# Attention in 64x64 blocks, local scores shelved by four transfers, and new orders: a four-layer attention kernel on one core

## The chip, the core and the metric

The kernel runs on one core of a Trainium2 chip. A core has five engines that work side by side, each through its own list of instructions in order: PE (matrix products, with PEld for the loading of weights), DVE and ACT (elementwise work and reductions), POOL (slower elementwise work) and SP, which does nothing here but issue DMA transfers. Data lie in DRAM, in an on-chip memory of 128 partitions (SBUF), and in eight banks that PE writes and DVE and ACT read (PSUM). The metric is the device time of one execution in microseconds (us), the median of several runs; less is better.

## What is computed

Four residual layers follow each other on one sequence of 2048 positions and 512 channels, in 32 heads of 16 channels: A, B, A, B. Layer A is local: each query sees 8 keys, at its own position and at every second position before it. Layer B is a causal window of 256 keys.

```python
    def _A_ref(x, wqkv, wo):
        B, S, D = x.shape
        H = 32; Dh = D // H
        W, dil = 8, 2
...
        off = jnp.arange(W) * dil
        idx = pos[:, None] - off[None, :]
        mask = idx >= 0
...
        logits = jnp.einsum("bhsd,bhswd->bhsw", q, kg) * scale
        logits = jnp.where(mask[None, None, :, :], logits, -1e9)
        attn = _softmax(logits, axis=-1)
        o = jnp.einsum("bhsw,bhswd->bhsd", attn, vg)
        return (lambda x, *d: x.transpose(*d))(o, 0, 2, 1, 3).reshape(B, S, D) @ wo

    def _B_ref(x, wqkv, wo):
        B, S, D = x.shape
        H = 32; Dh = D // H; W = 256
...
        scores = jnp.einsum("bhqd,bhkd->bhqk", q, k) * (Dh ** -0.5)
        idx = jnp.arange(S)
        mask = (idx[:, None] - idx[None, :] >= 0) & (idx[:, None] - idx[None, :] < W)
        scores = jnp.where(mask[None, None], scores, -1e9)
        p = _softmax(scores, axis=-1)
        o = jnp.einsum("bhqk,bhkd->bhqd", p, v)
        return (lambda x, *d: x.transpose(*d))(o, 0, 2, 1, 3).reshape(B, S, D) @ wo

    x = A_x
    x = x + _A_ref(_layernorm(x, axis=-1), A_wqkv, A_wo)
    x = x + _B_ref(_layernorm(x, axis=-1), B_wqkv, B_wo)
    x = x + _A_ref(_layernorm(x, axis=-1), A_wqkv, A_wo)
    x = x + _B_ref(_layernorm(x, axis=-1), B_wqkv, B_wo)
    return x
```

## The kernel before

The sequence is cut into 8 chunks of 256 positions. A pass takes a layer A and the layer B behind it through the chunks, so there are 16 periods, each with one chunk of A (`layer_a`) and one of B (`layer_b`); in time, A of the next chunk runs beside B of the last.

**Order.** The code doesn't run in the order in which it is written. Every step is added to a plan as a task with an engine, a price in us, the values that it reads and writes, and buffers with a count. A table `ORDER` has a place for every task, in its engine's list; a negative place moves the task to its other engine (`alt`, DVE instead of POOL for instance). `Plan.order()` replays these lists against the prices, and the instructions are recorded in the order that it gives. On the chip each engine takes its list strictly in order, SP too: a transfer that waits for data holds up all transfers behind it.

**Layer A, the way of the local scores.** PE computes for 32 queries at a time the scores against a window of 39 keys (L1153, the X tasks), for two halves t of the chunk. ACT copies them to a buffer `s` (L1161, two copies a half; the pool `psc` has two such buffers). `shelve` writes them to DRAM as `sd` (L1169), and `band` reads back only the 8 keys of each query (L1173, `l`), by a pitch that slides along the window. DVE takes the maximum (L1192), ACT the exponential, and the weights go out to DRAM (`ptd`, L1237) and come back spread (`pt`, L1243). PE mixes the values with them (L1260). In SP's list the read back stands behind its shelving and waits for its landing.

**Layer B.** Queries and keys of four 16-channel parts are stacked in tiles `stk`. For each quarter j of the heads there is first a pass for the row maxima: 8 units, each a score unit of 128 queries by 384 keys for two heads (L1354, L1357), a DVE step that folds the last 128 columns onto the first 128 through a triangular mask (`pick`, L1375), and a reduction over 256 columns (L1371). The maxima go through DRAM into `stk`, and the same products are made anew, transposed, with the maximum subtracted (L1447, L1449). For a group of four heads (`hh`, eight groups a chunk) and for each of the two key chunks b there are two score units, two exponentials of 128x768 on ACT (L1453) into a buffer `p` (pool `pp6`, three buffers), one POOL instruction that zeroes what lies outside the band (L1462), and eight products with the values (L1479) into one PSUM bank `acc`, which two groups share and ACT then copies out (L1515). In the first chunk of a layer there are no keys before it and half of this falls away. A key block is 128 keys against 256 queries, or 128 against 128, in which two corners of 64x64 are empty.

The lines of the shelving and of the read back; `sd.t` has 4 rows of 32 queries, `S_.t` 128 partitions of 39 x 32 numbers (`WIN` is 39, `H` 32):

```python
            def shelve(S_=S_, sd=sd):
                nc.sync.dma_start(sd.t[:, 0 : 32 * WIN * H].rearrange("g (q x) -> g q x", q=32), S_.t.rearrange("p k s -> p (k s)"))
...
            plan.add("SP", 0.4, shelve, r=vS, w=[vsd], size=650)
            plan.add("SP", 0.4, band, r=[vsd], w=[vL[t]], size=160)
```

## Time and profile before

| what | value |
|---|---|
| median of 3 runs | 1647.87 us (1644.64 to 1656.72) |
| the profiled execution, its time | 1659.09 us |
| its span, first to last instruction | 1657.3 us |
| mean granted clock of PE | 0.909 |
| PE's idle time by the span less its busy time | 271.4 us |

The profile is one execution. A row of a group says how long its instructions kept the engine busy, how long one took on average, and how long the engine stood idle just before them and for whom. The chain is the work that ended last, followed back from the end. A window's row has the busy time of each engine in a stretch, then the granted clock of PE (1.00 is full speed), the busy share of the 16 DMA engines and GB/s. PE in 40 slices of the span, its clock and the DMA share, in tenths:

```profile
PE   8779779699697978979698797978969799696987
...
PEclk9789999799798998989888898989979899797999
DMA  9665353444535446353354634545353564524341
```

The dips of PE come back once in two or three slices, that is once in a period of some 100 us.

### The profile page before, as it was taken

The page shows a single profiled execution, that of the slowest core. Times are in us where ns is not written, and L with a number is a line of the kernel's source. Part 1 is how long each engine was busy: PE and PEld are TensorE (multiplying, and loading weights), DVE is VectorE, ACT ScalarE, POOL GpSimd, SP SyncE. Part 2 cuts the span into 40 slices and gives each one's busy share as a digit, 9 for nine tenths or more (in the row PEclk, how much of TensorE's full clock was granted, in tenths as well). Part 3 has the DMA queues.
Part 4 walks back from the last instruction along what each step waited for, and adds up shares of the span by engine and source line. Part 5 has one row for each costly group of instructions (what it writes and reads, how often), then busy time and mean ns, then how long its engine had stood idle before and what let it go on. Part 6 is the DMA issues. An engine that isn't in the chain of part 4 may idle for free.

```text
span 1657.3 us, 49223 instructions
## 1 busy us (share of the span) xinstructions
PE 1385.9 (84%) x20958; PEld 840.1 (51%) x20958; DVE 856.1 (52%) x1768; ACT 879.8 (53%) x1343; POOL 408.6 (25%) x478
## 2 busy tenths in 40 slices
PE   8779779699697978979698797978969799696987
PEld 7555546356373554636355363644637356363533
DVE  7445464463645626365462526537453463545664
ACT  6533547366364654637465272755636465364554
POOL 4330113132031322213121031313222131121333
PEclk9789999799798998989888898989979899797999
DMA  9665353444535446353354634545353564524341
GB/s 267 166 138 144 103 120 90 126 119 127 130 105 122 114 132 116 117 147 108 91 118 125 136 103 139 119 129 124 109 111 96 142 131 121 135 80 124 81 118 54
DMA packets 181397, 202.09 MB, mean 122 GB/s; under 512 B 90269, under 2 KB 120733, under 8 KB 181177
## 3 DMA queue, kind: packets, MB, share of 16 engines
q1 hardware_dynamic: 180920, 198.68, 46.4%
q8 instruction: 164, 2.69, 0.7%
q14 instruction: 57, 0.46, 0.1%
q10 hardware_dynamic: 256, 0.26, 0.1%
HBM read 101.97 MB, written 79.36 MB: 109 GB/s over the span
## 4 chain that ended last, share of the span: by engine, by line
PE 49%; DMA 28%; DVE 6%; issue 5%; SPq 5%; ACT 5%; POOL 1%; ACTq 0%; POOLq 0%; DVEq 0%
DMA sd<-s 11%; PE banks L1007 7%; PE banks L1479 6%; PE banks L1008 6%; PE banks L1009 6%; PE banks L1029 4%; PE banks L1027 4%; DMA pt<-ptd 3%; PE banks L1030 3%; PE banks L1447 3%; PE banks L1153 2%; ACT p L1453 2%; PE banks L1354 2%; PE banks L1260 2%; DMA stk<-re 2%
## 5 line engine op out<-in xcount | busy, mean ns | idle before, releaser
L1453 ACT ACTIVATE p<-banks,sclB 128x768 f32<-128x768 f32 x480 | 415.8, 902 | 203.1 <-PE banks L1449 185.9
L1462 POOL TENSOR_SCALAR_AFFINE_SELECT p<-p 128x1024 f32<-128x1024 f32 x240 | 261.3, 1097 | 873.8 <-ACT p L1453 843.2
L1375 DVE COPY_PREDICATED banks<-maskt,banks 128x256 f32<-128x256 int16 x448 | 185.4, 425 | 238.1 <-PE banks L1357 208.0
L1371 DVE TENSOR_REDUCE m<-banks 128x2 f32<-128x512 f32 x448 | 302.7, 689 | 9.6
L1479 PE MATMUL banks<-p,v 128*32 128x256 f32 (+1 forms) x3840 | 206.5, 351 | 32.8 <-POOL p L1462 15.6
L1354 PE MATMUL banks<-stk,stk 48*128 48x128 f16 (+1 forms) x896 | 118.9, 261 | 85.2 <-DMA stk<-re 32.8
L1447 PE MATMUL banks<-stk,stk 64*128 64x256 f16 x960 | 132.4, 284 | 51.4 <-DVE m L1371 33.7
L1479 PEld LDWEIGHTS banks<-p,v 128*32 128x32 f32 x3840 | 113.4, 115 | 118.2 <-issue 55.6
L1357 PE MATMUL banks<-stk,stk 48*128 48x256 f16 (+1 forms) x1024 | 131.5, 258 | 14.1 <-DMA stk<-re 5.9
L1354 PEld LDWEIGHTS <-stk 48*128 48x128 f16 x896 | 51.7, 96 | 179.2 <-issue 120.7
L1447 PEld LDWEIGHTS <-stk 64*128 64x128 f16 x960 | 55.6, 95 | 126.2 <-issue 92.0
L1291 DVE SCALAR_TENSOR_TENSOR el<-banks,eh 128x512 f16<-128x512 f32 x64 | 43.1, 689 | 126.5 <-ACT eh L1288 88.4
L1449 PE MATMUL banks<-stk,stk 64*128 64x128 f16 x960 | 107.2, 222 | 0.0
L1192 DVE TENSOR_REDUCE mx<-l 128x64 f32<-128x512 f32 x32 | 32.9, 1027 | 137.5 <-DMA l<-sd 99.1
L1260 PE MATMUL banks<-pt,vs 39*32 39x64 f32 x4096 | 62.9, 251 | 39.2 <-DMA pt<-ptd 19.5
L1161 ACT COPY s<-banks 128x624 f32<-128x624 f32 x64 | 74.7, 1260 | 38.6 <-PE banks L1153 38.6
L1260 PEld LDWEIGHTS banks<-pt,vs 39*32 39x32 f32 x4096 | 52.6, 114 | 50.1 <-issue 28.6
L1008 PE MATMUL banks<-xl,wA1h 128*128 128x256 f16 x256 | 70.8, 277 | 1.0 <-issue 1.0
L1007 PE MATMUL banks<-xh,wA1h 128*128 128x256 f16 x256 | 70.9, 277 | 0.4 <-DMA xh<-ht 0.4
L1007 PE MATMUL banks<-xh,wA0h 128*128 128x256 f16 x256 | 71.2, 278 | 0.1
L1007 PE MATMUL banks<-xh,wB0h 128*128 128x256 f16 x256 | 71.2, 278 | 0.0
L1008 PE MATMUL banks<-xl,wA0h 128*128 128x256 f16 x256 | 71.0, 277 | 0.0
(202 smaller groups left out, 2851.3 us busy)
## 6 DMA issues: line engine op xcount, KB each, us to landing
stk<-re SPq DMA_DIRECT2D x256, 96.0 KB
sd<-s SPq DMA_DIRECT2D x32, 624.0 KB
pt<-ptd SPq DMA_DIRECT2D x64, 312.0 KB
re<-eh SPq DMA_DIRECT2D x128, 128.0 KB
vs<-vd SPq DMA_DIRECT2D x64, 156.0 KB
vd<-ve SPq DMA_DIRECT2D x32, 256.0 KB
xm<-y SPq DMA_DIRECT2D x32, 256.0 KB
re<-el SPq DMA_DIRECT2D x64, 128.0 KB
```

Source lines behind the costliest of these rows:

```text
L1007: nc.tensor.matmul(ps[mp].t[:, i], wh, xh, start=k == 0, stop=False)
L1008: nc.tensor.matmul(ps[mp].t[:, i], wh, xl, start=False, stop=False)
L1260: nc.tensor.matmul(acc.t[32 * r : 32 * r + 32, bb].rearrange("p (a x q u) -> p a x q u", a=2, q=16, u=2)[:, :, 2 * m + b2], vs.t[k, b2, 32 ...
L1354: nc.tensor.matmul(ps.t[:, par, 0 : (2 - qb) * P], lhs, stk[hf, bef][r, col, qb * P :], start=True, stop=True)
L1357: nc.tensor.matmul(ps.t[:, par, (2 - qb) * P : 3 * P], lhs, stk[hf, now][r, col, : (1 + qb) * P], start=True, stop=True)
L1371: nc.vector.tensor_reduce(out=m.t[:, :, u, qb], in_=ps.t[:, :, 0 : 2 * P], op=ALU.max, axis=AX.X)
L1375: nc.vector.copy_predicated(t[:, :, 0:P], maskt[:, 0:P].bitcast(I16).unsqueeze(1).broadcast_to([P, 2, P]), t[:, :, 2 * P : 3 * P])
L1447: nc.tensor.matmul(o[:, two], k[:, jf * P : (jf + 1) * P], q, start=True, stop=True)
L1449: nc.tensor.matmul(o[:, one_], k[:, jo * P : (jo + 1) * P], q[:, qo * P : (qo + 1) * P], start=True, stop=True)
L1453: nc.scalar.activation(pt.t[:, :, 2 * i : 2 * i + 2].rearrange("p s m q -> p m s q"), ps.t[:, :, : 3 * P].rearrange("p m (s q) -> p m s q" ...
L1462: nc.gpsimd.affine_select(out=v, in_=v, pattern=[[0, 8], [-1 if b == 0 else 1, P]], compare_op=ALU.is_gt if b == 0 else ALU.is_ge, fill=0. ...
L1479: nc.tensor.matmul(o, v[:, jj, 17 * h : 17 * h + 32], rhs, start=z == 0 and (b == 0 or first), stop=z == 1 and b == 1, tile_position=(0, 3 ...
```

## The change

Three things change together.

1. `shelve` issues four transfers, one for each 32 partitions, instead of one. The pool `psc` goes from two buffers to one.
2. In chunks after the first, layer B works in blocks of 64 keys by 64 queries and leaves out those outside the band. A row-max unit runs over 320 columns for each 64 queries instead of 384 (`halves`), and the fold over 64 columns instead of 128. A group's scores come as two wide units of 448 columns and one thin unit, each PE instruction over a quarter of the array (64 rows by 64 columns); the exponentials become two of 128x896 and one of 128x768. The masks become two for a group, each either four POOL selects of 64x256 or one DVE copy. The values are 16 wide and 16 thin products on half the rows, into two banks, so that the two halves have to be added: one ACT copy and one DVE addition a group, instead of one ACT copy for two groups.
3. The table `ORDER` is another one throughout, and some prices of the plan are others: the shelving's, and that of the gather `get` (L1243), whose size goes from 1015 to 1350.

```diff
 ORDER = {
-    "S": [15, 11, 0, 1, 3, 2, 33, 16],
-    "pA": [2, -1, 3, -2, 2, 22, 4, 30, 8, 10, 11, 9, 10, 5, 8, 4, -4, 7, 31, 9, 39, 12, 32, -14, 16, 11, 15, 6, 13, 9,
...
+    "S": [16, 13, 12, 0, 11, 7, 6, 35, 19],
...
-    for name, bufs in (("px", 4), ("pqm", 1), ("pk", 1), ("psc", 2), ("pl", 1), ("ppt", 1), ("pvs", 1), ("pve", 1), ("po4", 1), ("pos", 2), ("pxn", 2),
-                       ("pxt", 2), ("pp6", 3), ("pqk", 2), ("poh", 2), ("ps1", 1), ("psm", 2)):
+    for name, bufs in (("px", 4), ("pqm", 1), ("pk", 1), ("psc", 1), ("pl", 1), ("ppt", 1), ("pvs", 1), ("pve", 1), ("po4", 1), ("pos", 2), ("pxn", 2),
+                       ("pxt", 2), ("pp6", 2), ("pp7", 2), ("pqk", 2), ("poh", 2), ("ps1", 1), ("psm", 2)):
...
             def shelve(S_=S_, sd=sd):
-                nc.sync.dma_start(sd.t[:, 0 : 32 * WIN * H].rearrange("g (q x) -> g q x", q=32), S_.t.rearrange("p k s -> p (k s)"))
+                for g in range(4):
+                    nc.sync.dma_start(sd.t[g, 0 : 32 * WIN * H].rearrange("(q x) -> q x", q=32), S_.t[32 * g : 32 * g + 32].rearrange("p k s -> p (k s)"))
...
-            plan.add("SP", 0.4, shelve, r=vS, w=[vsd], size=650)
+            plan.add("SP", 1.9, shelve, r=vS, w=[vsd], size=450)
...
+                    def halves(u=u, qb=qb, ps=ps, hf=hf, hp=hp):
+                        col = 4 * hp + u
+                        for part in range(2):
+                            for h in range(2):
+                                for par in range(2):
+                                    r = slice(64 * par, 64 * par + 48)
+                                    n = C - qb * P - 64 * h
+                                    lhs = stk[hf, 0][r, col, qb * P + 64 * h : qb * P + 64 * h + 64]
+                                    o = ps.t[64 * h : 64 * h + 64, par, 0:320]
+                                    o, k = (o[:, 0:n], stk[hf, bef][r, col, C - n :]) if part == 0 else (o[:, n:], stk[hf, now][r, col, : 320 - n])
+                                    nc.tensor.matmul(o, lhs, k, start=True, stop=True, tile_position=(64 * par, 64 * h))
...
                     def pick(ps=ps):
                         t = ps.t
-                        nc.vector.copy_predicated(t[:, :, 0:P], maskt[:, 0:P].bitcast(I16).unsqueeze(1).broadcast_to([P, 2, P]),
-                                                  t[:, :, 2 * P : 3 * P])
+                        nc.vector.copy_predicated(t[:, :, 0:64], trm[:, 0].bitcast(I16).unsqueeze(1).broadcast_to([P, 2, 64]), t[:, :, C : C + 64])
...
+                def score(ps, at, i, pieces, hh=hh, hf=hf):
+                    col = 2 * (hh % 4) + i
+                    for n in range(2):
+                        for h in range(2):
+                            for par in range(2):
+                                r = slice(64 * par, 64 * par + 64)
+                                kt, k0, q0, q1, x0 = pieces[h][n]
+                                nc.tensor.matmul(ps.t[64 * h : 64 * h + 64, par, at + x0 : at + x0 + q1 - q0], stk[hf, kt][r, col, k0 : k0 + 64],
+                                                 stk[hf, 0][r, col, q0:q1], start=True, stop=True, tile_position=(64 * par, 64 * h))
+
+                wide_ = (((now, 0, 0, 256, 0), (bef, 128, 0, 192, 256)), ((bef, 192, 0, 256, 192), (now, 64, 64, 256, 0)))
+                thin_ = (((now, 128, 128, 256, 0), (bef, 0, 0, 64, 128)), ((bef, 64, 0, 128, 64), (now, 192, 192, 256, 0)))
...
+                def mask(E, x, n):
+                    if E is nc.vector:
+                        v = x.t[:, :, 0:64]
+                        p, m, z = (list(y) for y in v.ap)
+                        v = bass.AP(tensor=v.tensor, offset=v.offset, ap=[p, m, [n - 64, 2], z])
+                        E.copy_predicated(v, trm[:, 1:3].bitcast(I16).unsqueeze(1).broadcast_to([P, 4, 2, 64]),
+                                          nul.unsqueeze(1).unsqueeze(1).broadcast_to([P, 4, 2, 64]))
+                        return
+                    for h in range(2):
+                        r = slice(64 * h, 64 * h + 64)
+                        for v, a, op in ((x.t[r, :, 0:64], 1, ALU.is_ge), (x.t[r, :, n - 64 :], -1, ALU.is_gt)):
+                            E.affine_select(out=v, in_=v, pattern=[[0, 4], [a, 64]], compare_op=op, fill=0.0, base=0, channel_multiplier=-a)
...
+                plan.add("POOL", 1.5, lambda E, f=mask, x=big: f(E, x, 448), r=[*vbig, vtri], w=[vm2], mode="S", alt=("DVE", 0.65))
+                plan.add("POOL", 1.5, lambda E, f=mask, x=small: f(E, x, 192), r=[vsmall, vtri], w=[vs2], mode="S", alt=("DVE", 0.65))
+
+                acc = Banks(psum, 2, [P, 2, 512])
...
+                def value(x, pieces, begin, hh=hh, acc=acc):
+                    for n in range(2):
+                        for mm in range(4):
+                            for h in range(2):
+                                r = slice(64 * h, 64 * h + 64)
+                                vv, blk, x0, q0, q1 = pieces[h][n]
+                                hd = 8 * mm + hh
+                                nc.tensor.matmul(acc.t[32 * mm : 32 * mm + 32, h, q0:q1], vv[r, blk, 17 * hd : 17 * hd + 32], x.t[r, mm, x0 : x0 + q1 - q0],
+                                                 start=begin and n == 0, stop=not begin and n == 1, tile_position=(64 * h, 32 * mm), skip_group_check=True)
+
+                wide2 = (((va, 0, 0, 0, 256), (vb, 1, 256, 0, 192)), ((vb, 1, 192, 0, 256), (va, 0, 0, 64, 256)))
+                thin2 = (((va, 1, 0, 128, 256), (vb, 0, 128, 0, 64)), ((vb, 0, 64, 0, 128), (va, 1, 0, 192, 256)))
+                vals = [*vvt[c % 3], *vvt[(c - 1) % 3]]
...
+                def both_(acc=acc, some=some):
+                    nc.vector.tensor_tensor(out=acc.t[:, 0, 0:C] if final else some(), in0=some(), in1=acc.t[:, 1, 0:C], op=ALU.add)
+
+                vhf = Val(os_[hf])
+                plan.add("ACT", 0.3, lambda acc=acc, some=some: nc.scalar.copy(some(), acc.t[:, 0, 0:C]), r=[vacc], w=[vhf])
```

In the last chunk of the last layer the division by the sum of the weights is done for each group instead of for two. Two small constants (`trm`, `nul`) are set on POOL at the start.

What the new orders make of it is shown at two places. The first is SP's list at the ninth period (layer A of the second pass, first chunk): `sd_0_0` and `sd_0_1` are the two halves of the shelved scores, `l` the read back, `stk<-re` the stacked queries and keys of layer B, `vd` and `vs` the values of layer A, `md` the row maxima. Before:

```order
L1312 DMA stk_0_129<-re_7_0_10160 48x1x1024 x2
L1169 DMA sd_0_0_10461<-s_0_0_10438 4x32x1248
L1312 DMA stk_0_132<-re_7_0_10160 48x1x1024 x2
L1173 DMA l_0_10566<-sd_0_0_10461 64x2x256
L1223 DMA vd_0_147<-ve_0_0_10481 128x512
L1169 DMA sd_0_1_10592<-s_0_1_10553 4x32x1248
L1232 DMA vs_0_0_10605<-vd_0_147 39x2x512 x2
L1173 DMA l_0_10566<-sd_0_1_10592 64x2x256
L1408 DMA md_7_0_10655<-mt_7_0_10640 4x32x32 x2
```

and now, on the same list:

```order
L1434 DMA stk_0_135<-md_6_3_12848 2x1024 x2
L1176 DMA sd_0_0_12961<-s_0_0_12928 32x1248 x4
L1230 DMA vd_0_152<-ve_0_0_12980 128x512
L1651 DMA oc_6_13035<-os_6_0_12127 16x1024 x4
L1319 DMA stk_0_135<-re_7_0_12582 48x1x1024 x2
L1239 DMA vs_0_0_13144<-vd_0_152 39x2x512 x2
L1180 DMA l_0_13165<-sd_0_0_12961 64x2x256
L1176 DMA sd_0_1_13195<-s_0_1_13131 32x1248 x4
L1428 DMA md_7_0_13256<-mt_7_0_13248 4x32x32 x2
L1180 DMA l_0_13165<-sd_0_1_13195 64x2x256
L1319 DMA stk_0_135<-re_7_0_12582 48x1x1024 x2
```

Between the first half and its read back there were two transfers, now nine; between the second half and its own there were two and still are. Over all 32 shelvings it is 4.7 issues on average before and 6.6 now.

The second place is PE's list where it multiplies weights and values of one group (`p` and `ps` are the wide and the thin weights, `v` the values). Before, two units of eight products:

```order
L1027 LDWEIGHTS ol_7_9609
L1027 MATMUL banks<-wA3h,ol_7_9609 128x512
L1479 MATMUL banks<-p_6_1_0_9603,v_137 32x256 x4
L1479 MATMUL banks<-p_6_1_0_9603,v_137 32x128 x4
L1479 MATMUL banks<-p_6_1_1_9773,v_135 32x256 x4
L1479 MATMUL banks<-p_6_1_1_9773,v_135 32x128 x4
```

and now the end of a wide part and the beginning of its thin part, in which each second product is for the other half of the rows:

```order
L1583 MATMUL banks<-p_7_2_13910,v_139 32x256
L1583 MATMUL banks<-p_7_2_13910,v_138 32x256
L1583 MATMUL banks<-p_7_2_13910,v_138 32x192
L1583 MATMUL banks<-p_7_2_13910,v_139 32x192
L1583 MATMUL banks<-p_7_2_13910,v_138 32x192
L1583 MATMUL banks<-p_7_2_13910,v_139 32x192
L1583 MATMUL banks<-p_7_2_13910,v_138 32x192
L1583 MATMUL banks<-p_7_2_13910,v_139 32x192
L1583 MATMUL banks<-p_7_2_13910,v_138 32x192
L1583 MATMUL banks<-p_7_2_13910,v_139 32x192
L1583 MATMUL banks<-ps_7_2_13807,v_139 32x128
L1583 MATMUL banks<-ps_7_2_13807,v_138 32x128
```

A group has 16 products before and 32 now, over half the rows each. On PE's whole list the kind of tile changes 1096 times before and 1061 times now.

More of the change, by code (lines that the diff above doesn't have):

```diff
@@ L1514, in evict @@
-            def evict(hp=hp, hf=hf, acc=acc):
-                nc.scalar.copy(flat(os_[hf]).rearrange("p (g t) -> p g t", g=4)[:, 2 * hp : 2 * hp + 2], acc.t)
-            plan.add("ACT", 0.49, evict, r=[vacc], w=[vos[hf][hp]])
+                big = buf("pp6", [P, 4, 448], F32, "p6", f"p{l}_{c}_{hh}")
+                small = buf("pp7", [P, 4, 192], F32, "p7", f"ps{l}_{c}_{hh}")
+                vbig, vsmall = [Val(big), Val(big)], Val(small)
+                need = [vst[hf, 0, hp], vst[hf, "m", hp], vst[hf, now, hp], vst[hf, bef, hp]]
```

197 lines of the change are left out of this document (123 added, 74 removed), and 777 rows, old and new, of the table ORDER.

## The prediction, made before the changed kernel was run

> **What bounds the kernel now.** I read the page first, then the waits of the DMA queue SP, then one disturbed place in order of time, then the chain, then two tables of windows. The page's row of busy time, and the longest of SP's own waits:
>
> ```profile
> PE 1385.9 (84%) x20958; PEld 840.1 (51%) x20958; DVE 856.1 (52%) x1768; ACT 879.8 (53%) x1343; POOL 408.6 (25%) x478
> ```
>
> ```profile
> SPq L1173 <- DMA sd<-s: 133.6, 28, 10.3
> ```
>
> PE is the busiest engine, but 16% of it is idle. The second row says where to look: SP, which issues everything in order, stands 133.6 us on the landing of the local scores (`sd<-s`, the shelving) before it may issue the read back (`l<-sd`). One such place in order of time, on SP, on ACT and on PE:
>
> ```profile
> 798.02 0.59 SPq L1169 DMA_DIRECT2D sd<-s  x1
> 798.65 2.49 SPq L1312 DMA_DIRECT2D stk<-re  x2
> 808.39 0.56 SPq L1173 DMA_DIRECT2D l<-sd  x1
> 809.05 0.55 SPq L1223 DMA_DIRECT2D vd<-ve  x1
> 809.69 0.59 SPq L1169 DMA_DIRECT2D sd<-s  x1
> 813.08 1.84 SPq L1232 DMA_DIRECT2D vs<-vd  x2
> 820.78 0.56 SPq L1173 DMA_DIRECT2D l<-sd  x1
> ```
>
> ```profile
> 801.16 2.34 ACT L1161 COPY s<-banks 128x624 f32<-128x624 f32 x2 [1.08 <-PE banks L1153]
> ```
>
> ```profile
> 825.26 1.51 PE L1479 MATMUL banks<-p,v 128*32 128x256 f32 x16 [9.64 <-POOL p L1462]
> ```
>
> Shelving is issued at 798.02 and again at 809.69, and SP comes to the read 10.4 and 11.1 us later. What stands behind it is late, and PE is idle for 9.64 us before 825.26. Now the chain, as a whole and at one period:
>
> ```profile
> core 0 of [0], span 1657.3 us
> by line: DMA sd<-s 10.6%; PE banks L1007 6.5%; PE banks L1479 6.2%; PE banks L1008 6.0%; PE banks L1009 5.9%; issue 5.3%; PE banks L1029 3.8%; PE banks L1027 3.6%; DMA pt<-ptd 3.5%; PE banks L1030 3.3%; PE banks L1447 2.7%; PE banks L1153 2
> ```
>
> ```profile
> 705.62 11.68 DMA sd<-s
> 717.32 2.60 DMA l<-sd
> ...
> 724.91 3.32 DMA ptd<-bands
> ```
>
> Shelving is its largest single item: 10.6% of 1657.3 us, 176 us, in 14 pieces like the one shown, 12.6 us each on average. The next rows are windows; their last two numbers are the busy share of the DMA engines and GB/s.
>
> ```profile
> 803.00:806.50 3.50, 3.25 (x32) 1.33 (x26) 2.89 (x6) 2.46 (x4) 1.10 (x1) 1.00 0.26 86
> 810.00:810.90 0.90, 0.90 (x28) 0.52 (x20) 0.87 (x3) 0.29 (x1) 0.00 (x0) 1.00 1.06 376
> ```
>
> While shelving runs nearly alone (803 to 806.5) the 16 DMA engines are 26% busy and move 86 GB/s; with other transfers (810) they are full and move 376. So a shelving of 624 KB keeps about four engines busy (0.26 x 16) and twelve idle.
>
> [...]
>
> Two tables of windows follow, shortened to their first and last rows and their sums.
>
> ```profile
> 192.00:222.00 30.00, 19.65 (x269) 10.41 (x267) 12.14 (x24) 10.65 (x14) 5.17 (x6) 0.83 0.33 100
> ...
> 1493.00:1524.00 31.00, 18.64 (x301) 8.38 (x295) 12.28 (x23) 11.95 (x15) 4.37 (x4) 0.78 0.35 108
> sum 377.00, PE 226.93 PEld 111.29 DVE 146.55 ACT 152.07 POOL 67.75; mean PE 16.21 PEld 7.95 DVE 10.47 ACT 10.86 POOL 4.84
> ```
>
> ```profile
> 222.00:297.00 75.00, 66.26 (x1160) 43.39 (x1158) 35.60 (x69) 46.68 (x69) 20.52 (x23) 0.97 0.42 108
> ...
> 1421.00:1493.00 72.00, 68.23 (x1083) 43.61 (x1080) 42.64 (x81) 41.06 (x63) 17.67 (x18) 0.95 0.44 107
> sum 955.00, PE 884.92 PEld 556.31 DVE 522.55 ACT 562.48 POOL 241.94; mean PE 68.07 PEld 42.79 DVE 40.20 ACT 43.27 POOL 18.61
> ```
>
> The first takes 14 stretches, each from a first shelving to some 6 us behind the second read; the other the 13 stretches between. Around the shelvings PE is busy 227 of 377 us at a granted clock of 0.83 (mean of the 14 rows, weighted by length); elsewhere 885 of 955 us, 93%, at 0.94. So outside the shelvings the kernel is bound by PE, inside by the way of the local scores through DRAM.
>
> **The change part by part.** *Shelving by four transfers.* Each shelving becomes four issues of 156 KB. The nearest rows are the two above: 128 KB read back in 2.60 us, 144 KB written to DRAM in 3.32. Three further issues at 0.64 (809.05 to 809.69) add 1.9, so the last quarter lands 4.5 to 5.2 us after the first issue; I take 5.2, from the row that writes. If nothing spreads, it stays as it was and the issues add 14 x 1.9 = 27. **A**: 14 x 5.2 = 73 against 176 on the chain, -103. The single buffer for the scores (psc 2 to 1) makes the second copy wait for the first landing: 5.2 + 2.34 (the two copies) + 5.2 = 12.7 us from first issue to second landing, where the place above took 22.8 (798.02 to 820.78); it stays below. SP gets 96 more issues, 96 x 0.6 = 58 us, which A holds where they matter. In the new order 6.6 issues on average stand between the last piece of a shelving and its read, 4.7 before, so more of the landing is covered.
>
> *The clock.* **B**: PE's 227 us in the stretches at 0.94 instead of 0.83 are 200, so -27. The rows show the low clock beside idle PE, and A takes the idleness away.
>
> *PE's work.* In later chunks each key-query product runs over 640 columns where it ran over 768: 5/6 of the columns, in tiles of half the height, with twice as many instructions. The prices, from PE's rows in order of time at three places:
>
> ```profile
> 810.70 0.23 PE L1354 MATMUL banks<-stk,stk 48*128 48x128 f16 x2
> 810.77 0.27 PE L1357 MATMUL banks<-stk,stk 48*128 48x256 f16 x2
> 810.88 0.28 PE L1447 MATMUL banks<-stk,stk 64*128 64x256 f16 x2
> ```
>
> ```profile
> 332.47 1.60 PE L1260 MATMUL banks<-pt,vs 39*32 39x64 f32 x128
> 334.00 0.39 PE L1029 MATMUL banks<-wB2h,xh 128*128 128x512 f16 x1
> ```
>
> ```profile
> 792.24 0.86 PE L1479 MATMUL banks<-p,v 128*32 128x256 f32 x16
> ...
> 801.36 1.51 PE L1479 MATMUL banks<-p,v 128*32 128x256 f32 x32
> ```
>
> A score unit takes 0.18 us (810.70 to 810.88), a value unit (16 records) 1.51 - 0.86 = 0.65. Per group of four heads there were 4 row-max units, 4 score units and 2 value units: 0.72 + 0.72 + 1.30 = 2.74 us. Now there are 4 row-max units of 0.15 (0.18 x 5/6), score units of 0.21, 0.21 and 0.18 (by columns), and values of 1.30 x 5/6 = 1.08 by columns, of which the wide part has 448 in 640, 0.76, and the thin one 0.32. The thin part has 32 records; at the mixing's pace, 1.53 us for 128, they need 0.38, which I take. Sum 0.60 + 0.60 + 1.14 = 2.34, 0.40 less; in 112 groups (8 in each of 14 chunks) 45, and at PE's 93% share **C** = -42. This supposes that tiles of half height run together as those of full height do. The mixing has such tiles (39 rows by 32 columns, in both halves of the rows): its 128 records of 64 columns took 1.53 us, where four at a time at the value unit's pace (0.65 us for 3,072 columns) would take 1.73. The other end: values at the mixing's 1.53/8192 us a column, 1.91 a group for 10,240, would make it 3.11 a group, +41. I take the first end, because the mixing's records are too short to be bound by their columns.
>
> [...]
>
> *ACT, DVE, POOL.* The groups of instructions that change:
>
> ```profile
> L1453 ACT ACTIVATE p<-banks,sclB 128x768 f32<-128x768 f32 x480 | 415.8, 902 | 203.1 <-PE banks L1449 185.9 <-PE banks L1479 4.6 <-POOL p L1462 2.7
> ...
> L1462 POOL TENSOR_SCALAR_AFFINE_SELECT p<-p 128x1024 f32<-128x1024 f32 x240 | 261.3, 1097 | 873.8 <-ACT p L1453 843.2 <-issue 18.1 <-ACT mt L1395 4.8
> ...
> L1375 DVE COPY_PREDICATED banks<-maskt,banks 128x256 f32<-128x256 int16 x448 | 185.4, 425 | 238.1 <-PE banks L1357 208.0 <-ACT s L1161 11.4 <-PE banks L1449 8.6
> ```
>
> ACT: four exponentials of 0.90 a group become two of at most 1.05 (0.90 x 896/768) and one of 0.90, plus a copy of half an accumulator: some 50 us less in all. I give it nothing, since ACT already waits 186 us for PE at that line. DVE: 448 picks over half the columns take between 0.21 and 0.43, say 0.30, -56; 112 new additions of at most 0.43 add 48, and 82 masks that moved from POOL, each over twice the columns of the pick, at most 0.85, add up to 70. Together up to +62; it hides under PE, DVE being busy 523 of 955 us in the second table, and costs that if the cover is gone. POOL loses 224 selects of 1.10 (246 us) and gets 142 masks of four small selects, by size a quarter of 1.10 each at least, so 156 us and more. A value unit waits for a mask, with two wide and two thin buffers ahead of it: nothing. The accumulator now takes two PSUM banks for one group instead of one for two: nothing, while eight banks carry three score units beside it; its cost is the first rival's. The order on PE changes between kinds of tile 1061 times, before 1096: nothing.
>
> *Sum.* By the chain -103 - 27 - 42 = -172, a span of 1485. By PE instead of A: if the stretches' idle time falls from 150 of 377 us to the 7% of elsewhere, 28, that is -122 - 27 - 42 = -191, a span of 1466. The middle is 1476; with the 1.8 us by which the profiled run (1659.1) exceeds its span, 1478. The median of the three runs, 1647.9, is 0.9932 of the profiled run: **1468**.
>
> **The rivals.** *Another wait takes the place.* Half of A and B go to what stands next: SP with its 58 us of issues, the banks of the accumulator, or the way from the read to the mixing (2.60, 3.32 and the gather). That is -52 - 13 - 42 = -107, so 1541 on the median, to 1570 if half of the issues come on top. For it speaks that the local scores still pass through DRAM twice; against it, that SP's longest wait is the one that goes.
>
> *The records are the bound.* If those of the new tiles come no closer than 24 ns, twice the mixing's 12, the thin scores (16 records) take 0.38, the wide ones still 0.21 each, the row max 0.19 each and the values 64 x 0.024 = 1.54: 3.10 a group, +0.36 instead of -0.40, so 85 us more, 79 at PE's share: 1547. For it speaks that the instructions double and get shorter; against it the mixing's pace.
>
> *It doesn't do what it says.* If quarters land as late as the whole, A and B vanish, and A may be +27: 1659 - 42 = 1617 to 1644, on the median 1606 to 1633. The 0.26 speaks against it.
>
> *Slower.* Row halves that don't overlap: with as many tiles at once as before, values cost 1.08 x 2 = 2.17, scores and row max 1.20 each, 4.57 a group, +1.83, 205 us against A and B of -130. That is +75, 1722 on the median. It turns to a loss from 130/112 = 1.16 us a group on. The mixing's 1.53 us speaks against it.
>
> **How the numbers follow.** The forecast has 0.72, the next wait 0.14, the records 0.05, no effect of the split 0.05, no overlap 0.04. The likeliest case alone lies between 1390 and 1530. Low end: the stretches run at the pace of elsewhere (200 + 885 - 45 = 1040 us of PE in 14 periods, at 93% 1118 instead of 1332, so -214, or -237 over 15.5 periods, 1412), and the clock rises too. High end: A and C, each a little short, without B. The range to hold 8 in 10 takes in the first two rivals: 1390 to 1570. About 1% is what a measurement of this kernel can tell from no change: faster 0.94, within 1% 0.02 (the far end of no effect), slower 0.04.
>
> **What would show it.** A: SP's wait for `sd<-s` falls from 133.6 us to below 50, its share of the chain from 10.6% to under 5%, and a read comes 4 to 7 us after the first issue. B: the stretches' clock rises from 0.83 towards 0.94. C: a wide value part lasts 0.76 us until its successor, a thin one 0.38. It would be wrong if the read still waits 10 us, if the values of a group take over 1.4 us, or if PE's idle time moves to the gather `pt<-ptd`, to `stk<-re` or to the single buffer of the scores.

## The result, and the profile after

The changed kernel takes 1537.3 us (median of 4 runs, 1533.0 to 1548.0) where the kernel before, run beside it, takes 1646.9: the ratio is 0.933, 95% interval 0.927 to 0.940. In a second measurement it is 0.928 (0.925 to 0.931). The forecast was 1468 us, 0.891. The sign and most of the mechanism are as forecast, but a gain of 180 us was forecast and 110 came. The experiments below show that this is not one term a little short: two of the three terms came in full, and the third came with the opposite sign.

First the rows that answer to those shown of before. The page's row of busy time, and its chain by engine and by line, of the kernel after:

```profile
PE 1352.3 (88%) x28126; PEld 870.6 (57%) x28126; DVE 869.0 (57%) x1966; ACT 829.8 (54%) x1301; POOL 386.9 (25%) x828
```

```profile
PE 55%; DMA 16%; DVE 10%; issue 7%; SPq 7%; ACT 5%; POOL 1%; DVEq 0%; ACTq 0%; POOLq 0%
PE banks L1583 7%; PE banks L1013 7%; PE banks L1014 6%; PE banks L1015 6%; PE banks L1033 4%; PE banks L1035 4%; DMA pt<-ptd 4%; PE banks L1377 4%; PE banks L1036 4%; PE banks L1528 4%; PE banks L1267 3%; DVE m L1392 3%; PE banks L1159 2%; DMA sd<-s 2%; SPq L1308 2%
```

Shelving (`sd<-s`) has 2% of the chain, where it had 10.6%. But PE is busy for 1352 us, where it was busy for 1386: the span fell by 124 us, and PE's busy time by only 34.

The same place in order of time as was shown of before (start, duration, then engine and line), on SP and on ACT, after:

```profile
824.03 2.73 SPq L1176 DMA_DIRECT2D sd<-s  x4
...
832.29 2.89 SPq L1176 DMA_DIRECT2D sd<-s  x4
835.23 0.56 SPq L1180 DMA_DIRECT2D l<-sd  x1
...
837.59 0.55 SPq L1180 DMA_DIRECT2D l<-sd  x1
```

```profile
828.98 2.26 ACT L1167 COPY s<-banks 128x624 f32<-128x624 f32 x2 [1.75 <-DMA sd<-s]
```

The second read is issued 5.3 us after its shelving's first issue; before it was 11.1. The second copy on ACT waits 1.75 us for the first shelving to land, as the single buffer makes it. SP's own wait for the landing, after:

```profile
SPq L1180 <- DMA sd<-s: 9.4, 14, 2.1
```

It was 133.6 us. Now the two tables of windows, after: the 14 stretches around the shelvings, bounded as before, and the 13 between (span of the window, busy us of PE, PEld, DVE, ACT and POOL, granted clock, DMA share, GB/s).

```profile
175.00:194.00 19.00, 18.72 (x348) 10.23 (x348) 11.91 (x24) 11.84 (x17) 4.60 (x5) 0.82 0.57 152
...
1368.00:1395.00 27.00, 21.43 (x538) 11.98 (x540) 19.10 (x43) 13.49 (x19) 7.80 (x20) 0.91 0.63 169
sum 288.00, PE 247.89 PEld 133.62 DVE 167.22 ACT 144.26 POOL 75.45; mean PE 17.71 PEld 9.54 DVE 11.94 ACT 10.30 POOL 5.39
```

```profile
194.00:261.00 67.00, 60.16 (x1386) 41.95 (x1378) 38.61 (x79) 39.04 (x62) 11.45 (x22) 1.00 0.49 115
...
1296.00:1368.00 72.00, 66.05 (x1513) 45.82 (x1506) 40.47 (x85) 36.33 (x56) 16.23 (x38) 0.93 0.47 108
sum 932.00, PE 841.22 PEld 561.11 DVE 515.93 ACT 523.34 POOL 234.12; mean PE 64.71 PEld 43.16 DVE 39.69 ACT 40.26 POOL 18.01
```

PE's idle time in the stretches fell from 150 us to 40 (288 - 248), and their clock, weighted by length, rose from 0.83 to 0.92. Between them it rose from 70 us to 91 (932 - 841). These rows show where the idleness went. They don't show why PE's work shrank so little, nor whether the Block layer's new tiles helped at all.

### The profile page after: what moved, and what is told of

Its sections match the earlier page's. It is cut to its first block, busy times and chain, and to the rows that moved or that the text cites. A ratio compares the mean times of both kernels' runs of the same rounds, so it can differ in the third digit from the quotient of the medians.

```text
span 1533.4 us, 64202 instructions
## 1 busy us (share of the span) xinstructions
PE 1352.3 (88%) x28126; PEld 870.6 (57%) x28126; DVE 869.0 (57%) x1966; ACT 829.8 (54%) x1301; POOL 386.9 (25%) x828
## 4 chain that ended last, share of the span: by engine, by line
PE 55%; DMA 16%; DVE 10%; issue 7%; SPq 7%; ACT 5%; POOL 1%; DVEq 0%; ACTq 0%; POOLq 0%
PE banks L1583 7%; PE banks L1013 7%; PE banks L1014 6%; PE banks L1015 6%; PE banks L1033 4%; PE banks L1035 4%; DMA pt<-ptd 4%; PE banks L1377 4%; PE banks L1036 4%; PE banks L1528 4%; PE banks L1267 3%; DVE m L1392 3%; PE banks L1159 2%; DMA sd<-s 2%; SPq L1308 2%
## 5 line engine op out<-in xcount | busy, mean ns | idle before, releaser
L1538 ACT ACTIVATE p<-banks,sclB 128x896 f32<-128x896 f32 x224 | 221.3, 1006 | 77.4 <-PE banks L1528 62.1
L1396 DVE COPY_PREDICATED banks<-trm,banks 128x128 f32<-128x128 int16 x448 | 125.4, 291 | 150.6 <-PE banks L1377 142.6
L1377 PE MATMUL banks<-stk,stk 48*64 48x192 f16 (+3 forms) x3584 | 147.8, 249 | 49.1 <-DMA stk<-re 15.7
L1567 POOL TENSOR_SCALAR_AFFINE_SELECT p<-p 64x256 f32<-64x256 f32 x296 | 116.7, 416 | 271.4 <-ACT p L1538 258.9
L1567 POOL TENSOR_SCALAR_AFFINE_SELECT ps<-ps 64x256 f32<-64x256 f32 x272 | 109.3, 423 | 255.9 <-ACT ps L1550 251.1
L1377 PEld LDWEIGHTS <-stk 48*64 48x64 f16 x3584 | 83.0, 111 | 141.8 <-issue 117.3
L1528 PE MATMUL banks<-stk,stk 64*64 64x128 f16 (+3 forms) x3584 | 126.8, 245 | 22.8 <-ACT p L1538 7.7
L1583 PE MATMUL banks<-p,v 64*32 64x192 f32 (+1 forms) x3584 | 129.9, 386 | 9.6 <-issue 6.0
L1550 ACT ACTIVATE ps<-banks,sclB 128x768 f32<-128x768 f32 x112 | 100.1, 899 | 50.5 <-PE banks L1528 36.1
L1167 ACT COPY s<-banks 128x624 f32<-128x624 f32 x64 | 74.5, 1263 | 60.2 <-DMA sd<-s 32.6
L1583 PEld LDWEIGHTS banks<-p,v 64*32 64x32 f32 x3584 | 68.6, 113 | 46.7 <-issue 24.0
L1583 PE MATMUL banks<-ps,v 64*32 64x64 f32 (+1 forms) x3584 | 77.0, 260 | 12.2 <-issue 12.1
L1583 PEld LDWEIGHTS banks<-ps,v 64*32 64x32 f32 x3584 | 69.1, 112 | 22.5 <-issue 18.4
```

Source lines behind the costliest of these rows:

```text
L1377: nc.tensor.matmul(o, lhs, k, start=True, stop=True, tile_position=(64 * par, 64 * h))
L1396: nc.vector.copy_predicated(t[:, :, 0:64], trm[:, 0].bitcast(I16).unsqueeze(1).broadcast_to([P, 2, 64]), t[:, :, C : C + 64])
L1528: nc.tensor.matmul(ps.t[64 * h : 64 * h + 64, par, at + x0 : at + x0 + q1 - q0], stk[hf, kt][r, col, k0 : k0 + 64], stk[hf, 0][r, col, q0: ...
L1538: nc.scalar.activation(big.t[:, 2 * i : 2 * i + 2], ps.t[:, :, 0:448], AF.Exp, scale=scl["B", 1])
L1550: nc.scalar.activation(small.t.rearrange("p (i m) x -> p m i x", i=2), ps.t[:, :, 0:384].rearrange("p m (i x) -> p m i x", i=2), AF.Exp, s ...
L1567: E.affine_select(out=v, in_=v, pattern=[[0, 4], [a, 64]], compare_op=op, fill=0.0, base=0, channel_multiplier=-a)
```

## The experiments

Each kernel was timed against the kernel before on the same chip; ratios are to that one. "Four transfers" is the new shelving.

**1. The shelving alone, and everything but the shelving.** The first puts the new shelving into the kernel before, with its old order, old tiles and two score buffers:

```diff
-                nc.sync.dma_start(sd.t[:, 0 : 32 * WIN * H].rearrange("g (q x) -> g q x", q=32), S_.t.rearrange("p k s -> p (k s)"))
+                for g in range(4):
+                    nc.sync.dma_start(sd.t[g, 0 : 32 * WIN * H].rearrange("(q x) -> q x", q=32), S_.t[32 * g : 32 * g + 32].rearrange("p k s -> p (k s)"))
```

> The kernel before with one edit: each shelving of the local scores is issued as four transfers of 32 partitions. The prediction on record puts A and B there, -103 to -122 and -27 of the span, so about 1518 us (ratio 0.92). What the trace after shows instead: PE's idle time in the shelve stretches fell by 110 us (150 to 40) and its clock gained little, so about 1540 (0.935), nearly all of the change's effect, with the Block layer's part near nothing. Rival, the new orders carry it: the old order can't use the earlier landing, 1600 or more (0.97). In the trace SP's wait for the landing should fall from 133.6 us to below 30 by the first two.

Measured: 0.9115 (0.908 to 0.915), and in a second measurement

> The kernel before with the shelving in four transfers, again, beside its two variants on the same chip: 0.908 to 0.915.

0.914 (0.912 to 0.916). This one edit makes the kernel faster than the whole change does. My reading of the trace after (1540 us, 0.935) was wrong, and the sum of A and B on record (about 1518, 0.92) was close, a little too slow. The row of SP's wait, the page's row of busy time, and the sums of the same two tables of windows, for this kernel:

```profile
SPq L1174 <- DMA sd<-s: 15.3, 22, 2.1
```

```profile
PE 1357.1 (90%) x20958; PEld 830.3 (55%) x20958; DVE 857.6 (57%) x1768; ACT 879.6 (58%) x1343; POOL 408.7 (27%) x478
```

```profile
sum 246.00, PE 211.56 PEld 106.16 DVE 139.33 ACT 146.55 POOL 67.14; mean PE 15.11 PEld 7.58 DVE 9.95 ACT 10.47 POOL 4.80
```

```profile
sum 961.00, PE 877.06 PEld 553.14 DVE 530.58 ACT 568.33 POOL 242.62; mean PE 67.47 PEld 42.55 DVE 40.81 ACT 43.72 POOL 18.66
```

The stretches shrink from 377 us to 246, their idle time from 150 to 34, and their clock is 0.98. The second kernel is the opposite: the changed kernel with the shelving as one transfer again (the edit above, the other way round).

> The changed kernel with one edit: the shelving is one transfer again. If the split carries nearly all, about 1630 us (0.99 of the kernel before), with SP waiting over 100 us for the landing. If the Block layer and the new orders carry half of the gain, about 1590 (0.965). If the orders hide a late landing, under 1570.

Measured: 1.026 (1.021 to 1.030), with SP waiting 99.9 us for the landing. Without the new shelving, the rest of the change makes the kernel slower than it was before. All three expectations had it too fast. In the new order the split is worth 1.026 - 0.928, about 10% of the kernel before; in the old one 8.7%.

**2. Why four transfers land early: the spread, or the number?** Four transfers again, cut the other way, in the kernel before:

```diff
+                for g in range(4):
+                    n = WIN * H // 4
+                    nc.sync.dma_start(sd.t[:, 0 : 32 * WIN * H].rearrange("g (q x) -> g q x", q=32)[:, :, g * n : g * n + n],
+                                      S_.t.rearrange("p k s -> p (k s)")[:, g * n : g * n + n])
```

> The kernel before with the shelving in four transfers that are cut the other way: each has all 128 partitions (the shape 4x32 rows) and a quarter of the columns, so as many issues and bytes as with four transfers of 32 partitions. If what counts is how a transfer is spread over the DMA engines (four groups outermost, four engines), it lands as late as before and the 14 x 1.9 us of issues come on top: 0.99 to 1.02. If what counts is the number of issues, it lands early: 0.91 to 0.93.

Measured: 0.998 (0.996 to 1.000): nothing gained. The waits of SP, two shelvings with their reads, and a window inside the first, of this kernel; then two shelvings with their reads, and windows inside both, of the kernel with four transfers by partitions:

```profile
SPq L1176 <- DMA sd<-s: 97.2, 35, 5.5
```

```profile
794.12 2.63 SPq L1171 DMA_DIRECT2D sd<-s  x4
804.39 0.56 SPq L1176 DMA_DIRECT2D l<-sd  x1
805.63 2.54 SPq L1171 DMA_DIRECT2D sd<-s  x4
816.32 0.59 SPq L1176 DMA_DIRECT2D l<-sd  x1
```

```profile
799.00:803.00 4.00, 3.60 (x36) 1.61 (x36) 3.13 (x6) 2.96 (x4) 1.10 (x1) 1.00 0.32 106
```

```profile
731.47 1.96 SPq L1170 DMA_DIRECT2D sd<-s  x4
735.88 0.56 SPq L1174 DMA_DIRECT2D l<-sd  x1
...
737.12 2.42 SPq L1170 DMA_DIRECT2D sd<-s  x4
741.92 0.57 SPq L1174 DMA_DIRECT2D l<-sd  x1
```

```profile
732.50:735.00 2.50, 2.50 (x154) 2.02 (x154) 1.73 (x5) 1.42 (x2) 0.24 (x1) 1.00 1.04 273
737.50:740.50 3.00, 3.00 (x28) 1.25 (x27) 2.74 (x7) 2.39 (x5) 1.44 (x2) 1.00 0.92 277
```

Cut by columns, the 16 DMA engines stay about a third busy (0.32) and the reads follow 10.3 and 10.7 us after the first issue; cut by partitions they are full, together with the other transfers of that stretch (1.04, 0.92), and the reads follow after 4.4 and 4.8. The number of issues is the same, so the number is not the cause. The pieces cut by columns also have rows a quarter as long; but the single transfer, with whole rows, had the DMA engines just as idle (0.26) and landed as late. What is left is the spread: 0.26 and 0.32 of 16 engines are four and five for the one shape, with four groups outermost, and 0.92 and 1.04 are 15 and all 16 for the other, with 32 rows outermost, the other transfers of each window included. What in a shape decides on the number of engines is not shown beyond these shapes.

**3. What the Block layer's part is worth.** The changed kernel beside the parts:

> The changed kernel as it is, beside the runs of its parts on the same chip: 0.928 to 0.940 of the kernel before. Against 0.9115 for the four transfers alone, the Block layer's new tiles and the new orders would then cost 1.5% to 3%, where the prediction on record had them gain 42 us.

Measured: 0.928 (0.925 to 0.931), against 0.9115 and 0.914 for the four transfers alone. What the Block layer's tiles, their buffers and the new orders add is a loss of about 1.6% of the time, some 24 us (by the first measurement, 0.933, some 34). To see where, PE's time is divided (worked out from the trace): each matmul counts from its start to the next one's, at most its own duration and 0.02 us, as us at full clock (at half clock half of it counts); the other half is "lost to half clock", and the rest is idle. The 5 to 6 us ahead of the first matmul and behind the last are in the span alone. "Code limits" is the part of the idle time that stands ahead of one instruction in each 256 of PE's stream; it is explained under 4.

```
us                    before  four    after   after   four, half  four, more  after, whole
                              transf.         again   row max     records     row max
row max               121.7   124.3   124.4   124.9   128.3       122.5       138.9
scores                116.8   118.4   103.2   102.1   125.7       114.9       111.9
values                179.5   180.4   164.8   167.4   180.4       193.4       163.2
other PE work         872.4   877.9   876.2   876.2   872.6       876.9       878.0
lost to half clock     99.8    60.5    88.0    86.3    77.4        69.5        76.4
idle                  261.4   144.7   171.2   170.7   146.0       146.2       162.1
  of it, code limits   30.6    26.7    59.6    69.3    34.1        33.2        49.1
span                 1657.3  1511.9  1533.4  1533.1  1536.2      1529.2      1536.1
```

A column is one execution. A second profile of the four transfers alone (span 1509.0) has 30.5 us at code limits, 69 lost to half clock and 140 idle, so rows of two kernels that differ by less than some 10 us in these three can't be told apart.

From "four transfers" to "after", PE's work at full clock falls by 32 us (scores 15, values 16, row max nothing). Idle time rises by 26 and the loss to half clock by 27; against the second profile it is 31 and 19. So the new tiles do save PE work, and more than all of it is given back.

**4. The tiles' instructions.** The change brings 7168 matmuls more, each with its weight load. Code reaches PE by DMA; the queue's rows on the page, before and then after (packets, MB, share):

```profile
q8 instruction: 164, 2.69, 0.7%
```

```profile
q8 instruction: 220, 3.60, 1.0%
```

56 packets more of 16,384 bytes each, for 14,336 instructions more: 256 instructions a packet. In the order of PE's matmuls, weight loads and semaphore instructions in the trace, PE's idle time is bunched at the place 193 of every 256: after, 59.6 of 171 us stand there, in 45 stops, and 0.4 us on the mean at each of the other 255 places; before, 30.6 of 261 us. Of the 49 gaps of over 0.25 us between starts there (after), 45 end 1.1 to 1.7 us after a code packet has landed. Such a stop can fall in the middle of a unit, with no wait for a semaphore in the trace. One of 1.90 us in order of time on PE, and PE's longest waits, after:

```profile
1322.77 0.35 PE L1267 MATMUL banks<-pt,vs 39*32 39x64 f32 x13
1325.01 0.31 PE L1267 MATMUL banks<-pt,vs 39*32 39x64 f32 x5 [1.90 <-issue]
```

```profile
PE banks L1267 <- DMA pt<-ptd: 18.4, 13, 3.4
PE banks L1583 <- issue: 18.1, 14, 2.8
PE banks L1159 <- issue: 16.5, 9, 3.9
PE banks L1377 <- DMA stk<-re: 15.7, 14, 2.5
PE banks L1377 <- DVE m L1392: 14.7, 28, 2.2
```

"Issue" is the page's word for a wait for nothing that it shows; two of the five longest are such, at the value units (L1583) and the local scores, where short records follow each other fast. All 59 us of PE's waits for "issue" after stand at this one place of the 256, and none elsewhere (worked out from the trace); before it is 22 of 25 us, with the four transfers alone 22, in their second profile 26. The other waits that stand there before end with something that the trace shows. The first test changes only the number of instructions. In the kernel before, each value record becomes two of half the columns (the second record of each pair begins its accumulation anew, so the values differ while the work is the same):

```diff
-                                nc.tensor.matmul(o, v[:, jj, 17 * h : 17 * h + 32], rhs, start=z == 0 and (b == 0 or first),
+                                for y in range(2):
+                                    n = P // 2 if z else P
+                                    nc.tensor.matmul(o[:, y * n : y * n + n], v[:, jj, 17 * h : 17 * h + 32], rhs[:, y * n : y * n + n] if z else rhs[:, y],
+                                                     start=z == 0 and (b == 0 or first), stop=z == 1 and b == 1, tile_position=(0, 32 * mm), skip_group_check=True)
```

> The kernel before with each value record split in two by columns (32 records a unit of 128 and 64 columns, not 16 of 256 and 128): the same columns, the same tiles of 128 rows, 7680 PE instructions more, 30 code fetches of 256 instructions. Theory, the supply of instructions: a unit inside a run keeps its 0.67 us, and PE's waits at every 256th instruction grow from 30.6 us by 15 to 35; time +5 to +25 us (1.003 to 1.015). Rival, a floor of 24 ns a record: the unit takes 0.77 us everywhere, +24 us, with the waits at every 256th instruction as before. Rival, neither: no change.

Measured: 1.007 (1.004 to 1.010). And with four transfers:

> The kernel before with the shelving in four transfers, and with each value record split in two by columns: the same columns and tiles, 7680 PE instructions more, 30 fetches. The second record of each pair begins its accumulation anew, which changes the values, not the work. Supply of instructions: 10 to 30 us over the kernel with four transfers alone, 0.918 to 0.930, with PE's waits at every 256th instruction up from 26.7 us by 10 or more; a value unit inside a run stays at 0.69 us. Rival, records cost nothing where the columns are the same: 0.9115.

Measured: 0.924 (0.921 to 0.926), 1.2% over the mean of the two measurements of four transfers alone. The size is as expected in both, the way only in part. The waits at code limits rose by 6 us each time, not by 10 or more (by those for "issue" alone from 22 to 36 us in the first kernel, and from 22 and 26 to 31 in the second); 13 us are the value units themselves (193.4 against 180.4 in the table): a unit inside a run takes 0.686 us instead of 0.674, but one that ends a run 0.84 instead of 0.79. The half clock takes 9 us more than in the first profile of the four transfers alone, and none more than in the second. A floor of 24 ns a record is excluded: 32 records in 0.686 us are 21 ns each.

The second test gives the row max back its whole tiles in the changed kernel, 3584 records fewer:

```diff
-                        plan.add("PE", 0.15, halves, r=[vst[hf, 0, hp], vst[hf, now, hp], vst[hf, bef, hp]], w=[vps], mode="Q", act=0.12)
+                        plan.add("PE", 0.15, scores, r=[vst[hf, 0, hp], vst[hf, now, hp], vst[hf, bef, hp]], w=[vps], mode="Q", act=0.12)
...
-                        nc.vector.copy_predicated(t[:, :, 0:64], trm[:, 0].bitcast(I16).unsqueeze(1).broadcast_to([P, 2, 64]), t[:, :, C : C + 64])
+                        nc.vector.copy_predicated(t[:, :, 0:P], maskt[:, 0:P].bitcast(I16).unsqueeze(1).broadcast_to([P, 2, P]), t[:, :, 2 * P : 3 * P])
```

> The changed kernel with the row-max units of later chunks as they were: tiles of 128 rows over 384 columns (4 records a unit, not 8) and the pick over 128 columns. The prediction on record prices this part of C at 0.12 us a group of four heads, 13 us in 112 groups: 1537 + 13 = 1550. The partition of PE's time shows no gain from it (135.1 us of row-max units before, 135.4 after), and 3584 records fewer are 28 fetches of 256 instructions fewer in 7168 instructions, 8 us at the mean stall of 0.27 us a fetch in the trace after: 1530 to 1540. VectorE gets 60 us more (448 x 0.134), which costs up to 15 if it isn't hidden: 1552.

Measured: 0.930 (0.927 to 0.933), between the two measurements of the changed kernel: nothing, on balance. The edit gives PE more work and VectorE 55 us more (924.0 against 869.0), and takes records away; the run doesn't tell how much each counts. The third test puts the half row max alone into the kernel with four transfers (the same lines the other way round, with the triangle mask made at the start):

> The kernel before with the shelving in four transfers, and with the changed kernel's row-max units in later chunks: tiles of half height over 320 columns (8 records a unit, not 4) and the pick over half the columns. Against the kernel with the four transfers alone (0.9115 of before, 1512 us). The prediction on record: 13 us less, 0.904. Supply of instructions: 448 units gain 0.013 us each (0.176 to 0.163, unit to unit, in the traces), 6 us, and 3584 records more are 28 fetches of 256 instructions more at 0.59 us (33 us of waits more in 56 more fetches, the changed kernel against the one with four transfers alone), 16 us: 10 us more, 0.915 to 0.921.

Measured: 0.928 (0.925 to 0.931), 1.6% over four transfers alone. This part, priced at -13 us, costs as much there as the Block layer's whole part does with its own orders. Both expectations fall. In the table the row max is 4 us dearer there, the score units between which it stands 7, the waits at code limits grow by 7, and 17 us go to half clock; against the second profile of the four transfers it is 5, 9, 4 and 8, and the old orders were made for other prices. In the new order the same tiles do save their 14 us of PE work (138.9 against 124.9) and the score units some 9, and the time doesn't show it: with whole tiles the idle time and the loss to half clock are 9 and 10 us smaller.

**5. Moving the code limits.** If the stops belong to the limits, moving all of PE's instructions by a few places moves the stops. A few of the filler matmuls at the start were taken out or added:

```diff
-            for _ in range(3):
+            for _ in range(2 if i < 47 else 3):
```

The second kernel has `4 if i < 5 else 3`; the third is the changed kernel with `2 if i < 95 else 3`.

> The kernel before with the shelving in four transfers, and 47 of the 330 filler matmuls at the start left out (they multiply the identity into unused banks while weights load), which moves every later PE instruction 94 places forward against the blocks of 256 in which code is fetched. Theory, supply of instructions: a block of 256 PE instructions takes at least 3.55 us. Worked out from the start times in the trace of the kernel with four transfers alone, the waits this makes come to 28.7 us at its own place of the block limits (measured 26.7), and to 14.4 us at the one 94 instructions on, the lowest of the 256. So PE's waits at block limits should halve to 12 to 18 us, and the time fall by 10 to 25 us with the clock that goes with them: 0.896 to 0.906. Rival, the waits belong to places in the program and not to block limits: 0.9115, waits as before.

> The same kernel with 5 filler matmuls more instead, 10 places the other way, at which the same sum comes to 37.4 us, the highest of the 256. Supply of instructions: waits at block limits 33 to 42 us, time 6 to 18 us over the kernel with four transfers alone, 0.915 to 0.922. Rival: 0.9115.

> The changed kernel with 95 filler matmuls at the start left out, 190 places. By the same sum its waits at block limits are 46.8 us at its own place (measured 59.6 and 69.3 in two profiles) and at least 39.4 anywhere: 56 fetches more can't be hidden by their place. So a little faster, by 5 to 20 us of 1536, 0.916 to 0.926, and still slower than the four transfers alone at their best place.

Measured: 0.9145 (0.911 to 0.918), 0.913 (0.911 to 0.915) and 0.922 (0.918 to 0.927). The 3.55 us for a block of 256 is the author's estimate, not a measured limit: the closest starts of two code packets are 3.33 us apart before and 3.34 after, and 4 of 163 and 10 of 219 come closer than 3.55. In the first the waits at the limits fell to 19.8 us (12 to 18 were expected), from 26.7 and 30.5 in two profiles without the edit, and what is left stands at place 193 of the moved count again, so they do go with the limits; but the time stayed, since PE waited as much in all (144 us) for other things. In the second neither moved (26.4 us, at the same place of the count), against the expectation. The third is inside its expected range, but its waits at limits fell only to 55 us, and 95 filler matmuls fewer are some 10 us of PE work at the start (0.109 us from one to the next in the trace after); it doesn't tell the two apart. So a us of waiting at a code limit is not a us of time: in the first of these kernels it went, and PE waited longer for other things.

## Why the prediction was right, and where it was wrong

The measured 1537 lies inside the stated range of 1390 to 1570, but in part by luck: the upper end was put there to take in two rivals, and neither happened as it was described. The likeliest case alone, in which C is a gain, was to end at 1530.

**A was right, in mechanism and size.** Four transfers kept 0.92 and 1.04 of the 16 engines busy (split alone, with the other transfers of those windows), where one kept 0.26 busy; that quarters of 32 partitions would spread so was the author's estimate, shown by no row of before. SP's wait for the landing fell from 133.6 us to 9.4 (below 50 was asked for), the chain's share to 2% (below 5%), and the second reads of a chunk come 4.2 to 7.2 us after their first issue in 15 of 16 chunks. The first reads, ahead of which SP now has other issues, come 5.5 to 16.2 us after theirs. By PE's idle time A was put at -122 us; with the split alone the stretches' idle time fell by 116 (150 to 34), the whole kernel's by 117.

**B was right.** With the split alone the stretches' clock went to 0.98, above the 0.94 that was taken, and the loss to half clock fell by 39 us over the kernel (30 in the second profile), where 27 were forecast for the stretches. A and B together were 130 to 149 us of the span; measured, 8.6% to 8.9% of 1647.9 are 142 to 146.

**C was wrong: -42 was forecast, and the part costs some 24 us.** Most prices held, and the step from work to time failed. With more value units behind it, the wide value part takes 0.78 us (its 16 records of 256 columns 0.456, its 16 of 192 columns 0.325) against 0.76 forecast, the thin one 0.36 against 0.38; where other work comes next, as behind most thin parts, the thin one takes 0.52 until it starts. In a run of two groups, after, with the records that follow each run:

```profile
652.33 1.74 PE L1583 MATMUL banks<-p,v 64*32 64x256 f32 x64
654.09 0.38 PE L1035 MATMUL banks<-wB2h,xh 128*128 128x512 f16 x1
...
654.61 1.07 PE L1583 MATMUL banks<-ps,v 64*32 64x128 f32 x64
655.62 0.39 PE L1033 MATMUL banks<-wB2h,xl 128*128 128x512 f16 x1
```

Two wide parts take 1.76 us and two thin ones 1.01, the change of tile at each end included. Scores saved 15 us where 13 were forecast, values 16 of 18; only the row max, 13 us, gave nothing (0.163 us from unit to unit where 0.15 was taken and 0.176 measured before, and nothing where a unit stands alone). That leaves 32 of 45 us of PE work. The step that failed is the next one, "at PE's 93% share": it takes PE for the bound between the shelvings and lets its work become time. The runs show that it didn't: 32 us taken out came back as 26 us idle and 27 at half clock (31 and 19 by the second profile). In the changed kernel 21 us of PE work put back (whole row max) left the time as it was, though with 3584 records fewer. A busy share of 93% says how little is idle, not that PE alone sets the pace.

**Costed at nothing.** That ACT, VectorE and POOL hide their share was right as far as the runs go; their rows after:

```profile
L1538 ACT ACTIVATE p<-banks,sclB 128x896 f32<-128x896 f32 x224 | 221.3, 1006 | 77.4 <-PE banks L1528 62.1
L1396 DVE COPY_PREDICATED banks<-trm,banks 128x128 f32<-128x128 int16 x448 | 125.4, 291 | 150.6 <-PE banks L1377 142.6
L1567 POOL TENSOR_SCALAR_AFFINE_SELECT p<-p 64x256 f32<-64x256 f32 x296 | 116.7, 416 | 271.4 <-ACT p L1538 258.9
...
L1550 ACT ACTIVATE ps<-banks,sclB 128x768 f32<-128x768 f32 x112 | 100.1, 899 | 50.5 <-PE banks L1528 36.1
```

1.01 us for the wide exponential (1.05 forecast), 0.29 for the pick (0.30), 0.42 for a select of a quarter's size, where a quarter of 1.10 was the least. 55 us more on VectorE (whole row max) left the time as it was, in a run that changes PE's work too. SP's 96 issues more stand in the kernel with four transfers alone too, and didn't hurt it. What was left out altogether is the code: 7168 matmuls more were priced as PE time only, and 56 fetches of code were not in the sum.

**The rivals.** "Another wait takes the place" gave 1541, closest to the result, but for a reason that isn't there: no half of A and B was lost, neither to SP nor to the banks nor on the way to the mixing. "The records are the bound" at 24 ns is excluded for tiles such as these on separate parts of the array (21 ns in value units, and 16 records of 64 columns after follow each other in 0.14 us, 9 ns each). It was near the truth in one thing, that more and shorter records cost; the split records show 1.2% for 3840 of them. "No effect of the split" and "no overlap of row halves" are excluded by the runs under 1 and by the prices above.

**What stays open.** How the 24 us divide between code limits, clock and the new orders. The waits at the limits grew by 33 and 39 us in two pairs of profiles, more than the whole rise in idle time, but shifting the limits showed that such waits can be exchanged for others. All the new tiles in the old orders, and a second score buffer in the new ones, were not tried; neither is separated from the tiles. Behind the single buffer ACT waits 32.6 us for shelvings to land, where it waited for none before; whether any of it reaches PE is not shown.

## What to carry to other kernels

Before cutting work out of the busiest engine, ask whether the time follows that engine: a small known amount of work put back, as here the whole row max, is a first test, best with the number of instructions kept as it is. When a transfer lands late, look at the busy share of the DMA engines while it runs nearly alone; here a share of a quarter (0.26) told that the shape, not the size, was at fault, and cutting along the outermost dimension mended it. Two edits that come as one should be timed apart: the first alone is here the fastest kernel of all, 0.912 to 0.914 of the time before, 1.6% below the two together.

## What the runs showed of the hardware

*Code came as a stream with its own limit.* PE's code came in packets of 256 instructions, no two of which start less than 3.3 us apart (3.33 us before, 3.34 after), and at dense places PE stood at the limit: 59.6 us after, 30.6 before. After, PE passed some 175 of 220 limits without such a stop; the other 45 hold a third of its idle time.

*The clock was set window by window.* In both traces it is 1.00 or 0.50 of full speed and changes on a fixed grid of 3.41 us. The share of windows at half clock, by PE's busy share of the window before (worked out from the trace):

```
busy in the window before     under 0.5   0.5-0.7   0.7-0.9   0.9 and more
before, that one at full       35 of 36    5 of 21   0 of 57    0 of 271
before, that one at half       29 of 29    7 of 7    9 of 10    2 of 40
after, that one at full        19 of 22   10 of 40   3 of 63    0 of 254
after, that one at half          1 of 1    6 of 6   11 of 12    5 of 37
```

So waits of more than 1.7 us within one window, half of it, were nearly always followed by half clock in the next one (from full clock 35 of 36 before, 19 of 22 after), those of 1.0 to 1.7 us in 5 of 21 and 10 of 40, and PE mostly came back to full clock only after a window with 0.9 or more busy (38 of 40 and 32 of 37, against 1 of 10 and 1 of 12 at 0.7 to 0.9). So waits of 1 to 3 us, each small, went with lost clock here; the changed kernel loses 86 and 88 us at half clock in two profiles, where the four transfers alone lose 61 and 69.
